# A two-exponential wait becomes a one-exponential wait in front of a row half's first MLP matmul

## The chip, the cores and the metric

The kernel runs on one core of one Trainium2 chip. The metric is the device time of one execution in microseconds (us), the median of several runs. The engines are TensorE (PE, its weight loads shown as PEld), VectorE (DVE), ScalarE (ACT), GpSimd (POOL) and SyncE (SP, which issues the DMAs).

## What is computed

One transformer-like block over 2048 rows of width 512, all in float32. The layer-normed input goes two ways, and the two results are multiplied:

```python
xn = _layernorm(x)
qkv = xn @ wqkv                                # 32 heads of width 16
p = softmax(q @ k.T * 16 ** -0.5)              # per head, 2048 x 2048
s = (p @ v) @ wo
h = relu(xn @ w1 + b1) ** 2                    # 512 -> 1792
g = silu(h @ w2 + b2)                          # 1792 -> 512
out = x + s * g
```

## The kernel before

**Stages.** Layer norm and the q, k, v projections come first (until about 374 us of the profile). Then a loop runs over 512 steps (`NU * 16`). A step handles four heads, 512 queries and 128 keys: four score matmuls (line 1161, tile `se`) into a ring of three PSUM banks, four exponentials on ScalarE (line 1167, tiles `pt` and `ex`), and, two steps later, four matmuls of the exponentials with v (line 374, tile `po`), which the profile shows as eight. Sixteen steps make a unit; 32 units make the attention.

**Work beside it.** The softmax shift of a unit is taken from row maxima that are computed ahead of it: score matmuls of another orientation (line 300, tile `pm_t`, a ring of three banks) and a VectorE reduction for each (line 308, tile `mx`). The MLP and afterwards the `wo` projection are handed out to the steps as small pieces by the generator `dense()`. Float32 accuracy is kept by splitting each operand into a high and a low part and doing three matmuls per product (`terms3`).

**Row halves.** A score matmul contracts over 64 partitions only, so it uses one half of the PE's rows: half 0 (partitions 0 to 63) or half 1 (64 to 127). An MLP matmul contracts over 128, so it is cut in two, one for each row half, and both accumulate into the same PSUM bank `pd_t`. The kernel first issues all of one half's MLP matmuls, each beside a matmul of the attention on the other half, and then all of the other half's, with the roles swapped. [...]

**Long blocks.** From the second of eight MLP chunks on, most MLP pieces come as blocks of 12 units for each row half (`block`, line 228): one unit is two matmuls of 256 columns in the first layer (`first_pair`, weights `w1s`) or one of 512 columns in the second (`second`, weights `w2t`). `long_slots` spreads one block over four steps, two for each half, and writes PE's order out by hand: the PE, ScalarE, VectorE, GpSimd and SP queues all keep the order in which the code issues. `visit(h, mine, theirs)` reads two strings of letters, one for the half that does the MLP and one for the other: `D` is an MLP unit, `s` a score matmul with its exponential, `m` a row-maximum matmul with its reduction.

There are two forms of a half. If the row maxima are far enough ahead (`ahead_m`), it is `s`, 12 times `D`, `s`, then both steps' matmuls with v together. Otherwise it is 10 times `D`, a step's matmuls with v, then `D D s s`, then the other step's matmuls with v. The counters of the code give which form is used: of the 88 long blocks the first 54 take the first form, and the 34 from step 292 on take the second. In the profile the second form runs from about 1020 us to 1478 us.

**The recording.** In `visit`, each `s` of the half that has no `D` left is recorded in `last_use[0]`, so the last one stays. In the first form that is one exponential. In the second it is the second of the two behind the last `D`.

**Who uses it.** In each of the 34 blocks the first MLP matmul of half 1. Where the block does not end its accumulation (13 of the 34), the recorded exponential is also used by the first MLP matmul of the next block, or of the next single slot (`halves`, line 190; three of the 13). Where it ends it, `post` sends the bank to ScalarE (line 545: bias and relu of the first layer; line 566: copy of the second), `last_use[0]` is cleared, and the next block's first MLP matmul waits for that evacuation of the single bank `pd_t` instead.

Of the kernel before, what the change touches and what calls it, by code (L numbers as in the profile page):

```python
# [39 lines left out]
def kernel(  # L40
# [55 lines left out]
    with ExitStack() as ph:  # L96
# [80 lines left out]
        last_use = [None]  # L177
# [110 lines left out]
        def max_mm(j, spread=False):  # L288
            if not m_ready(j, 1):
                return None  # L290
            u, p, qb, kc = todo_m[j].pop(0)
            qd = u // 4
            if u not in mxs:
                mxs[u] = sp.tile([P, 16, 4], F32, name="mx")
            m_bank[0] += 1
            if spread and m_bank[0] % 2:
                ps = pe.tile([P, 512], F32, name="se")
            else:
                ps = pm.tile([P, 512], F32, name="pm_t")
            nc.tensor.matmul(  # L300
                ps,
                qms[u][p][64 * j : 64 * j + 64, qb * P : (qb + 1) * P],
                kas[qd, p][64 * j : 64 * j + 64, kc * 512 : (kc + 1) * 512],
                start=True, stop=True,
            )
            c = (2 * p + j) * 4 + qb
            done_m[j] += 1
            return nc.vector.tensor_reduce(  # L308
                mxs[u][:, c, kc : kc + 1], ps, axis=AX.X, op=ALU.max
            )  # L310
# [3 lines left out]
        def max_end():  # L314
            while steps[0] < sum(done_m) // 4:
                u, s = divmod(steps[0], 16)
                if s == 15 and min(done_m) < 32 * (u + 1):
                    return
                steps[0] += 1
                if s in (9, 11) and u + 1 < NU:  # L320
                    assert min(done_m) >= 32 * u + 16
                    load_q_pair(u + 1, "qm", (s - 9) // 2, qms.setdefault(u + 1, []))
                if s == 15:
                    m4 = sp.tile([P, 16], F32, name="m4")
                    nc.vector.tensor_reduce(m4, mxs[u], axis=AX.X, op=ALU.max)
                    mxs[u] = m4
                    late.append((now[0] + 2, u))

        def shift_due():
            if late and late[0][0] <= now[0]:  # L330
                shift(late.pop(0)[1])
# [821 lines left out]
        def exp_mm(st, j, pts, spare):  # L1153
            u, kb = divmod(st, 16)
            qd = u // 4
            b = 64 * (j % 2)
            if spare:
                se = pm.tile([P, 512], F32, name="pm_t")
            else:
                se = pe.tile([P, 512], F32, name="se")  # L1160
            nc.tensor.matmul(  # L1161
                se, kas[qd, j // 2][b : b + 64, kb * P : (kb + 1) * P],
                qes[u][j // 2][b : b + 64, :],
                start=True, stop=True,
            )
            pts[j] = free_pt.pop(0)
            return nc.scalar.activation(pts[j], se, AF.Exp, scale=0.25)  # L1167
# [3 lines left out]
        def pv_step(st, pts):  # L1171
            u, kb = divmod(st, 16)
            if kb == 0:
                pos[0] = pv.tile([P, 512], F32, name="po")
            pv_mm(pos[0], u // 4, kb, pts)
            free_pt.extend(t for _, t in sorted(pts.items()) if all(t is not x for x in gone_pt))
            if kb == NT - 1:
                if u < NU - 2:
                    evac(pos[0], u)
                elif u == NU - 2:  # L1180
                    unit_inner(pos[0])
                else:
                    unit_final(pos[0])
# [57 lines left out]
        def ahead_m(n, st):  # L1241
            wo0 = 16 * NU - 62
            for u in range(n // 64, NU):
                end = 16 * u - SHIFT
                n_max = n + 4 * max(0, end - st)
                n_max += max(0, min(end, wo0 + 32) - max(st, wo0))
                if n_max < 64 * (u + 1):
                    return False
            return True

        def long_slots(st0, units, post):

            todo = [[(st0 + k, j) for k in range(4) for j in (lane, lane + 2)] for lane in range(2)]
            for kb in range(st0, st0 + 4):
                pts.setdefault(kb, {})

            def s(lane):
                kb, j = todo[lane].pop(0)
                return exp_mm(kb, j, pts[kb], False)

            def visit(h, mine, theirs):
                own, other, use = units[h], 1 - h, None
                for i, ops in enumerate(zip(mine, theirs)):
                    for lane in (other, h):
                        o = ops[0] if lane == h else ops[1]
                        if o == "D":
                            own.pop(0)()
                        elif o == "m":
                            max_mm(lane)
                        elif o == "s":  # L1270
                            use = s(lane)
                            if lane == h and not own:
                                last_use[0] = use

            for h in range(2):
                st = st0 + 2 * h
                if st > st0:
                    begin(st)
                if ahead_m(sum(done_m) + 7, st + 2):
                    visit(h, "s" + "D" * 12 + "s", ".mmsmssmsmssmm")  # L1280
                    if h and post is not None:
                        post()
                    begin(st + 1)
                    max_end()
                    shift_due()
                    for kb in (st - 2, st - 1):
                        pv_step(kb, pts.pop(kb))
                else:
                    visit(h, "D" * 10, "msmsmsmsms")
                    max_end()  # L1290
                    shift_due()
                    pv_step(st - 2, pts.pop(st - 2))
                    begin(st + 1)
                    visit(h, "DDss", "mmsm")
                    if h and post is not None:
                        post()
                    max_end()
                    shift_due()
                    pv_step(st - 1, pts.pop(st - 1))
            if post is not None:  # L1300
                last_use[0] = None
            assert not todo[0] and not todo[1] and not units[0] and not units[1]
# [17 lines left out]
        def begin(st):  # L1320
            now[0] = st
            if st % 64 == 48 and st // 64 + 1 < NQ:
                load_v(st // 64 + 1)
            if st >= 64 and st % 64 < 6 and st // 64 + 1 < NQ:
                for n in range(2):
                    load_k(st // 64 + 1, 2 * (st % 64) + n)
            u, s = divmod(st + 16, 16)
            if 2 <= u < NU and s < 2:
                load_q_pair(u, "qe", s, qes.setdefault(u, []))
            run_waiting()  # L1330
# [56 lines left out]
```

## Time and profile before

| | |
|---|---|
| median of 3 runs | 1728.29 us (1727.36 to 1729.73) |
| the profiled execution | 1729.29 us |
| its span, first to last instruction | 1727.5 us |
| PE busy | 97% of the span |
| VectorE, ScalarE, GpSimd busy | 78%, 69%, 31% |
| granted TensorE clock, mean | 0.998 |

A line of the grouped views names the source line, the engine, the operation and the tiles (out<-in), then count, busy time and mean duration. In a timeline a row has the start in us from the span's start, the length, engine, line, operation, tiles, shapes and how many alike instructions were merged; in brackets stands how long that engine sat idle before and what released it. Matmuls are pipelined: a 512-column matmul is shown for 0.39 to 0.50 us although the next one of the same row half can start 0.23 us after it. So "busy" says that some matmul is in flight, not that both row halves are.

### The profile page before, as it was taken

Reading aid. Unit: us, or ns where it says so; the run is one execution under the profiler, and the core shown is the slowest. Engines: PE = TensorE matmul, PEld = TensorE weight load, DVE = VectorE, ACT = ScalarE, POOL = GpSimd, SP = SyncE. Lnnn points to the kernel's source line nnn. Section 1 sums busy time; section 2 is a strip of 40 time slices with the busy share of each in tenths; the row PEclk is TensorE's granted clock in tenths of the full one; section 3 lists DMA queues with packets and bytes.
Section 4 is the critical chain, followed back from the end, with each engine's and each line's share of the span. In section 5 each row is a group of like instructions: output and inputs, shape, how many; then the busy total and the mean of one; then the engine's idle time right before and its main releaser. Section 6 shows DMA issues by size and latency. Waiting matters only on the chain.

```text
span 1727.5 us, 35413 instructions
## 1 busy us (share of the span) xinstructions
PE 1671.6 (97%) x13296; PEld 997.1 (58%) x13296; DVE 1340.1 (78%) x2294; ACT 1194.8 (69%) x2354; POOL 528.9 (31%) x548
## 2 busy tenths in 40 slices
PE   6999999999999999999999999999999999999997
PEld 4766666556656655665665565555555555555533
DVE  6599988887787788778777877887788778888612
ACT  6211377778778777877787776676767766776585
POOL 4434567523212312321232122112310223133433
PEclk9999999999999999999999999999999999999999
DMA  7567455436232522553244333233315332157344
GB/s 275 168 214 232 168 174 171 118 93 164 59 98 88 129 75 69 149 118 88 61 130 93 87 112 88 77 100 92 96 56 118 87 104 54 38 188 204 101 146 137
DMA packets 156723, 208.00 MB, mean 120 GB/s; under 512 B 51272, under 2 KB 71240, under 8 KB 155016
## 3 DMA queue, kind: packets, MB, share of 16 engines
q1 hardware_dynamic: 156552, 205.74, 41.0%
q8 instruction: 105, 1.72, 0.4%
q14 instruction: 66, 0.54, 0.1%
HBM read 149.30 MB, written 56.09 MB: 119 GB/s over the span
## 4 chain that ended last, share of the span: by engine, by line
PE 84%; issue 4%; ACT 3%; POOL 2%; DVE 2%; DMA 2%; SPq 1%; POOLq 0%; ACTq 0%; DVEq 0%
PE po L374 24%; PE pd_t L234 17%; PE pm_t L300 14%; PE se L1161 12%; PE pd_t L202 6%; PE pd_t L936 2%; PE po L936 2%; DVE mx L308 2%; ACT pt L1167 2%; PE se L300 2%; PE se L967 1%; ACT r L545 1%; PE se L936 1%; PE po L967 1%; PE pd_t L967 1%
## 5 line engine op out<-in xcount | busy, mean ns | idle before, releaser
L308 DVE TENSOR_REDUCE mx<-pm_t 128x1 f32<-128x512 f32 x1946 | 1212.0, 682 | 266.0 <-PE pm_t L300 150.8
L1167 ACT ACTIVATE pt<-se 128x512 f32<-128x512 f32 x1721 | 909.7, 611 | 297.3 <-PE se L1161 213.7
L1161 PE MATMUL se<-qe,ka 64*128 64x512 f32 x1988 | 764.7, 423 | 2.0 <-ACT ex L1167 1.0
L300 PE MATMUL pm_t<-ka,qm 64*128 64x512 f32 x1946 | 737.9, 416 | 3.7 <-DVE mx L308 3.3
L374 PE MATMUL po<-pt,v 128*32 128x512 f32 x3562 | 522.2, 602 | 0.0
L300 PEld LDWEIGHTS pm_t<-ka,qm 64*128 64x128 f32 x1946 | 341.4, 184 | 215.3 <-DVE mx L308 198.2
L1161 PEld LDWEIGHTS se<-qe,ka 64*128 64x128 f32 x1988 | 352.7, 184 | 128.0 <-ACT pt L1167 56.8
L234 PE MATMUL pd_t<-xc,w1s 64*128 64x256 f32 x2352 | 317.7, 285 | 12.4 <-ACT r L545 11.4
L234 PEld LDWEIGHTS pd_t<-xc,w1s 64*128 64x128 f32 x2352 | 296.4, 187 | 25.4 <-ACT r L545 16.5
L234 PE MATMUL pd_t<-w2t,hT 64*128 64x512 f32 x936 | 247.5, 402 | 3.1 <-ACT r L545 2.4
L374 PE MATMUL po<-ex,v 128*32 128x512 f32 x534 | 204.8, 601 | 0.0
L1167 ACT ACTIVATE ex<-se 128x512 f32<-128x512 f32 x267 | 157.9, 611 | 54.3 <-PE se L1161 32.0
L374 PEld LDWEIGHTS po<-pt,v 128*32 128x32 f32 x3562 | 90.7, 108 | 157.2 <-issue 139.7
L234 PEld LDWEIGHTS pd_t<-w2t,hT 64*128 64x128 f32 x936 | 164.1, 184 | 20.7 <-issue 4.8
L548 POOL TENSOR_TENSOR r<-r 128x512 f32<-128x512 f32 x49 | 51.0, 1040 | 362.8 <-ACT r L545 362.7
L567 POOL TENSOR_TENSOR u<-u,b_t 128x512 f32<-128x512 f32 x16 | 20.6, 1286 | 301.2 <-ACT u L566 301.2
L202 PE MATMUL pd_t<-w2t,hT 64*128 64x512 f32 x408 | 105.6, 391 | 0.3
L412 POOL TENSOR_TENSOR ot<-ot,hl 128x512 f32<-128x512 f32 x31 | 39.8, 1283 | 199.1 <-DMA hl<-r_d 141.0
L202 PE MATMUL pd_t<-wot,oc 64*128 64x512 f32 x336 | 90.9, 406 | 8.7 <-DVE mx L308 6.2
L202 PEld LDWEIGHTS pd_t<-wot,oc 64*128 64x128 f32 x336 | 58.4, 184 | 58.3 <-ACT pt L1167 16.0
L308 DVE TENSOR_REDUCE mx<-se 128x1 f32<-128x512 f32 x102 | 69.6, 683 | 15.5 <-PE se L300 8.0
L202 PEld LDWEIGHTS pd_t<-w2t,hT 64*128 64x128 f32 x408 | 72.5, 184 | 10.7 <-issue 1.1
(125 smaller groups left out, 1227.8 us busy)
## 6 DMA issues: line engine op xcount, KB each, us to landing
w1s<-w_d SPq DMA_DIRECT2D x196, 256.0 KB
qm<-q_d SPq DMA_DIRECT2D x384, 32.0 KB
qe<-q_d SPq DMA_DIRECT2D x384, 32.0 KB
ka<-k_d SPq DMA_DIRECT2D x96, 128.0 KB
xn_d<-xT SPq DMA_DIRECT2D x8, 1024.0 KB
k_d<-hl SPq DMA_DIRECT2D x32, 256.0 KB
q_d<-hl SPq DMA_DIRECT2D x32, 256.0 KB
xc<-xn_d SPq DMA_DIRECT2D x16, 512.0 KB
```

What stands on the lines that cost most here:

```text
L202: mm = nc.tensor.matmul(out_, lh(r), rh(r), start=first_ and lane == 0, stop=last_ and lane == 1, skip_group_check=True,)
L234: mm = nc.tensor.matmul(out_, lh(r), rh(r), start=first_ and lane == 0, stop=last_ and lane == 1, skip_group_check=True,)
L300: nc.tensor.matmul(ps, qms[u][p][64 * j : 64 * j + 64, qb * P : (qb + 1) * P], kas[qd, p][64 * j : 64 * j + 64, kc * 512 : (kc + 1) * 512] ...
L308: return nc.vector.tensor_reduce(mxs[u][:, c, kc : kc + 1], ps, axis=AX.X, op=ALU.max)
L374: nc.tensor.matmul(po[32 * j : 32 * j + 32, :], vs[qd][:, (4 * kb + j) * VW : (4 * kb + j) * VW + 32], pts[j], start=(kb == 0), stop=(kb = ...
L412: nc.gpsimd.tensor_tensor(ot, ot, hl[:, 1].bitcast(F32), op=ALU.mult)
L548: nc.gpsimd.tensor_tensor(r, r, r, op=ALU.mult)
L567: nc.gpsimd.tensor_tensor(u, u, b2_t, op=ALU.add)
L936: nc.tensor.matmul(out_, lh(slice(0, P)), rh(slice(0, P)), start=first_, stop=last_)
L967: nc.tensor.matmul(out_, lh(slice(0, P)), rh(slice(0, P)), start=first_, stop=last_)
L1161: nc.tensor.matmul(se, kas[qd, j // 2][b : b + 64, kb * P : (kb + 1) * P], qes[u][j // 2][b : b + 64, :], start=True, stop=True,)
L1167: return nc.scalar.activation(pts[j], se, AF.Exp, scale=0.25)
```

## The change

Only the recording in `visit` changes. Behind the last `D`, the first `s` of that half is recorded and later ones are not. The order of instructions on every engine stays as it is.

```diff
             def visit(h, mine, theirs):
-                own, other, use = units[h], 1 - h, None
+                own, other, follow = units[h], 1 - h, True
                 for i, ops in enumerate(zip(mine, theirs)):
...
                         elif o == "s":
                             use = s(lane)
-                            if lane == h and not own:
-                                last_use[0] = use
+                            if lane == h and not own and follow:
+                                last_use[0], follow = use, False
```

## The prediction

> **What bounds the kernel now.** First the page and the two stages of the MLP, cut where the second form of a half begins.
>
> ```profile
> span 1727.5 us, 35413 instructions
> PE 1671.6 (97%) x13296; PEld 997.1 (58%) x13296; DVE 1340.1 (78%) x2294; ACT 1194.8 (69%) x2354; POOL 528.9 (31%) x548
> PE 84%; issue 4%; ACT 3%; POOL 2%; DVE 2%; DMA 2%; SPq 1%; POOLq 0%; ACTq 0%; DVEq 0%
> ...
> 374.00:1020.00 646.00, 642.57 (x5725) 397.19 (x5727) 512.12 (x873) 509.22 (x1019) 158.72 (x156) 1.00 0.37 100
> 1020.00:1478.00 458.00, 441.52 (x3647) 248.00 (x3640) 370.65 (x614) 322.30 (x635) 107.63 (x107) 1.00 0.33 89
> ```
>
> PE is the bound (97% busy, 84% of the chain), and in the stage that the change touches it shows 441.5 of 458 us busy. VectorE has 87 us to spare there, ScalarE 136. Read like this, at most 16 us of PE idle time are to be had. But busy means that one matmul is in flight; whether both row halves work is not in that number. So next the waits of PE's weight loads in the stage, and then a transition in order of time.
>
> ```profile
> PEld pd_t L234 <- ACT r L545: 16.5, 16, 1.0
> PEld pd_t L234 <- ACT pt L1167: 7.5, 24, 0.3
> PEld pd_t L234 <- ACT ex L1167: 1.6, 5, 0.3
> ```
>
> 29 times a weight load of an MLP matmul waits for an exponential, 0.3 us each. The change's wait is there, and it is not covered. Here is one, in the second layer:
>
> ```profile
> 1151.57 1.57 ACT L1167 ACTIVATE pt<-se 128x512 f32<-128x512 f32 x3 [1.34 <-PE se L1161]
> 1151.70 1.07 PE L374 MATMUL po<-pt,v 128*32 128x512 f32 x8
> 1152.69 0.50 PE L300 MATMUL pm_t<-ka,qm 64*128 64x512 f32 x1
> 1153.19 0.18 PEld L234 LDWEIGHTS pd_t<-w2t,hT 64*128 64x128 f32 x1 [0.32 <-ACT pt L1167]
> 1153.20 0.50 PE L234 MATMUL pd_t<-w2t,hT 64*128 64x512 f32 x1
> 1153.20 0.49 PE L1161 MATMUL se<-qe,ka 64*128 64x512 f32 x1
> 1153.54 0.39 PE L234 MATMUL pd_t<-w2t,hT 64*128 64x512 f32 x1
> ...
> 1155.37 0.39 PE L234 MATMUL pd_t<-w2t,hT 64*128 64x512 f32 x1
> 1155.69 0.64 PE L374 MATMUL po<-pt,v 128*32 128x512 f32 x4
> ```
>
> Three exponentials stand in ScalarE's queue: one of the other half, then the first and the second own one. They end at 1153.14. The matmuls with v (1151.70) are over; a row-maximum matmul, m1, starts on the one half at 1152.69; the MLP's first matmul, D1, starts on the other at 1153.20, 0.05 us after the last exponential. For 0.51 us one half of the array has no work, and PE counts as busy all the while, since m1 is shown for 0.50 us. Behind D1 in PE's queue stands the next score matmul, which comes out with it. From D1 on the ten MLP matmuls run at their own pace (1153.54 to 1155.37 is 8 x 0.23 us), and the next matmuls with v start 2.49 us after D1.
>
> **The change part by part.** Nothing is added, removed or reordered on any engine or DMA queue. 47 semaphore waits are lowered by one exponential: in each of the 34 blocks from step 292 on the first matmul of half 1, and 13 first matmuls of what follows a block that leaves its accumulation open. When the first own exponential ends is in the same rows: three took 1.57 us, one alone takes 0.60 (row below), so they end 0.49 us apart and the first own one at 1152.65. D1 could start at 1152.70, with m1. What that is worth differs by place: 29 plain ones, as the two waits count them; nine of the 34 in which a unit ends (every fourth block) and its transpose is in front; nine with a second wait.
>
> ```profile
> 1202.83 0.60 ACT L1167 ACTIVATE ex<-se 128x512 f32<-128x512 f32 x1 [1.40 <-PE se L1161]
> 1203.32 1.08 ACT L1167 ACTIVATE pt<-se 128x512 f32<-128x512 f32 x2
> 1203.96 0.50 PE L300 MATMUL pm_t<-ka,qm 64*128 64x512 f32 x1
> 1204.45 0.38 PE L234 MATMUL pd_t<-xc,w1s 64*128 64x256 f32 x1
> 1207.02 0.62 PE L374 MATMUL po<-pt,v 128*32 128x512 f32 x1
> ...
> 1189.71 1.58 ACT L1167 ACTIVATE pt<-se 128x512 f32<-128x512 f32 x3 [1.41 <-PE se L1161]
> 1191.20 0.50 PE L300 MATMUL pm_t<-ka,qm 64*128 64x512 f32 x1
> 1191.34 0.38 PE L234 MATMUL pd_t<-xc,w1s 64*128 64x256 f32 x1
> 1193.42 0.39 PE L1161 MATMUL se<-qe,ka 64*128 64x512 f32 x1
> 1193.92 0.64 PE L374 MATMUL po<-pt,v 128*32 128x512 f32 x4
> ```
>
> *First layer, D1 0.49 us behind m1: 15 places.* The two transitions above are a test that the kernel makes by itself. In the second, a transpose in front holds m1 back, so that D1 comes only 0.14 us behind it. From D1 to the matmuls with v it is 2.57 us in the one and 2.58 in the other: the stretch does not care how long D1 waited, it only begins later. The first own exponential ends at 1203.92 (1203.32 + 0.60), so D1 can start at 1203.97, 0.48 us earlier. 15 x 0.48 = 7.2 us.
>
> *First layer, 0.14 us behind: 4 places.* There the first own exponential is long done, and D1 goes with m1: 4 x 0.13 = 0.5 us.
>
> *Second layer, 0.50 us behind: 14 places.* The matmuls are longer here, and the attention's half becomes the later one. m5, the fifth row maximum of the stretch, needs the bank that m2's reduction frees:
>
> ```profile
> 1153.23 3.25 DVE L308 TENSOR_REDUCE mx<-pm_t 128x1 f32<-128x512 f32 x5 [0.24 <-PE pm_t L300]
> ...
> 1140.82 0.50 PE L300 MATMUL pm_t<-ka,qm 64*128 64x512 f32 x1
> 1140.96 0.50 PE L234 MATMUL pd_t<-w2t,hT 64*128 64x512 f32 x1
> 1143.47 0.64 PE L374 MATMUL po<-pt,v 128*32 128x512 f32 x4
> ```
>
> Five reductions take 3.25 us, 0.65 each at most, and m1's starts at 1153.23, 0.54 us behind m1, so m2's is over 1.84 us behind m1. m5 loads its weights then at the earliest, and a last score matmul follows it: in the first-layer place with 0.14 us, where this half already runs without the delay, that score matmul starts 2.22 us behind m1 (1193.42 less 1191.20). From the last matmul of a half to those with v it is 0.32 us (1155.37 to 1155.69). So they cannot start before 2.54 us behind m1. Now it is 3.00 (1152.69 to 1155.69): 0.46 us each, 14 x 0.46 = 6.4 us. The bound from the other side is the 0.14 us place of the second layer, 2.65 us (1140.82 to 1143.47); if nothing can get under that, it is 0.35 each.
>
> *Second layer, 0.14 us behind: 5 places.* 2.65 to 2.54 is 0.11 at best, 0 by the same doubt; 5 x 0.1 = 0.5 us.
>
> *Nine places with a second wait.* The first matmul of a block that follows an open accumulation, and of three single slots:
>
> ```profile
> 1109.89 1.08 ACT L1167 ACTIVATE pt<-se 128x512 f32<-128x512 f32 x2
> 1110.52 0.50 PE L300 MATMUL pm_t<-ka,qm 64*128 64x512 f32 x1
> 1111.12 0.47 PE L234 MATMUL pd_t<-w2t,hT 64*128 64x512 f32 x1
> ...
> 1113.58 0.63 PE L374 MATMUL po<-pt,v 128*32 128x512 f32 x3
> ...
> 1122.81 0.49 PE L1161 MATMUL se<-qe,ka 64*128 64x512 f32 x1
> 1123.40 0.47 PE L202 MATMUL pd_t<-w2t,hT 64*128 64x512 f32 x1
> ```
>
> D1 comes 0.60 us behind its neighbour, 0.15 us after the exponential's end (1110.97) instead of 0.05: a separate wait in PE's queue costs the 0.1, and it stays. The first own exponential ends at 1110.49, so D1 moves to 1110.64, 0.48 us. The start of the matmuls with v falls from 3.06 us behind m1 to 2.58, above the 2.54. 9 x 0.48 = 4.3 us (0.40 each if 2.65 is the floor).
>
> *The added wait.* A later score matmul that reuses the bank of the second exponential had that wait implied by D1's and now needs its own. It is the third one of the next stretch, over 1.2 us behind m1, and the exponential is done 0.45 us behind m1 (1153.14 less 1152.69): nothing, as long as it fits into the matmul. If it costs a separate wait each time, 47 x 0.1 = 4.7 us. The row above shows such a separate wait. [...]
>
> Sum: 7.2 + 0.5 + 6.4 + 0.5 + 4.3 = 18.9 us. Against the profiled execution's 1729.3 us that gives 1710.4. It lies 1.0 us over the median of the runs, 1728.3, from which it gives 1709.4.
>
> **What is late next.** VectorE's 87 spare us of this stage shrink to about 68, which still leaves it behind PE. At D1 of half 0 of the first layer the relu holds as before:
>
> ```profile
> 1209.02 1.58 ACT L1167 ACTIVATE pt<-se 128x512 f32<-128x512 f32 x3 [1.39 <-PE se L1161]
> 1210.46 0.85 ACT L545 ACTIVATE r<-pd_t,b_t 128x256 f32<-128x256 f32 x2
> 1211.37 0.38 PE L234 MATMUL pd_t<-xc,w1s 64*128 64x256 f32 x1 [0.71 <-ACT r L545]
> ```
>
> **The rivals.** *Given back at the relu.* 19 first-layer places are followed by this wait for the relu. If ScalarE were behind, it would end at the same time as before and swallow 7.7 of the 18.9 us: 1717.1 us. Against it: ScalarE sat idle for 1.39 us before those exponentials, waiting for PE, so the relu moves with PE.
>
> *Another wait ends at the same time.* If D1 were also held by something else that ends with the second exponential, the change would do nothing: 1728.3 us. Against it: D1 comes 0.05 us after ScalarE in the plain places, whether m1 is 0.14 or 0.49 us ahead.
>
> *Slower, by the clock.* [...] If the granted clock fell in this stage, its 441.5 us would stretch: at 0.94 by 28 us, so 1737 us. It decides at 18.9 / 441.5, a clock under 0.96. Against it: the stage before has PE at 642.6 of 646 us and a clock of 1.00. [...]
>
> **How the numbers follow.** The forecast, a gain of 12 to 21 us, 0.86; given back at the relu 0.08; no effect 0.03; slower by the clock 0.03. Likeliest 1709.4 us. Lower end: every delay goes whole, 29 x 0.50 + 9 x 0.14 + 9 x 0.60 = 21.2 us, 1707.1, and 1.1 us for the spread of the runs shown: 1706.0. Upper end: second layer at its floor (14 x 0.35, nothing for the five, 9 x 0.40) 4.9 + 3.6 + 7.7 = 16.2 us, less 4.7 for separate waits, is 1716.8; it takes the relu rival in: 1717.5. Faster by over 0.2% (3.5 us, about what a measurement of this kernel can tell from no change): 0.86 + 0.08 = 0.94; same 0.03; slower 0.03.
>
> **What the profile after would show.** The 29 waits for exponentials at line 234 gone from the weight loads; D1 within 0.02 us of m1 in the plain places and about 0.1 in the nine; from m1 to the matmuls with v about 2.58 us in the first layer and 2.54 in the second; PE's busy time of the stage down by some 18 us with its idle time hardly changed; the relu waits as long as before. The prediction is wrong if D1 still comes 0.05 us after ScalarE's last exponential, if relu or reduction waits grow by what D1 gained, or if the clock drops.

## The result, and the profile after

The changed kernel takes 1711.82 us (median of 4 runs, 1710.34 to 1712.72), against 1728.72 us (four runs of the kernel before, 1727.36 to 1729.73): ratio 0.9902, 95% interval 0.9885 to 0.9919. The profiled execution after took 1710.34 us, span 1708.6 us. That is 18.9 us less span than before.

First the head of the page, its chain line and the two stages of the MLP. The second stage, cut at 1478 us before, is cut at 1461 us here; the columns are stretch, length, busy time of PE, its weight loads, VectorE, ScalarE and GpSimd, granted clock, DMA share, GB/s.

```profile
span 1708.6 us, 35413 instructions
PE 1655.0 (97%) x13296; PEld 987.1 (58%) x13296; DVE 1337.6 (78%) x2294; ACT 1193.0 (70%) x2354; POOL 528.9 (31%) x548
PE 82%; issue 5%; ACT 3%; POOL 3%; DMA 3%; DVE 2%; SPq 1%; POOLq 0%; ACTq 0%; DVEq 0%
...
374.00:1020.00 646.00, 643.34 (x5729) 397.29 (x5729) 512.96 (x874) 509.94 (x1021) 158.82 (x156) 1.00 0.37 100
1020.00:1461.00 441.00, 425.42 (x3659) 238.57 (x3655) 368.66 (x615) 321.60 (x636) 107.62 (x107) 1.00 0.34 93
```

The stage without the change stands as it did. In the stage with it PE's busy time fell by 16.1 us (441.5 to 425.4) and its idle time from 16.5 to 15.6 us: the time came out of what the page calls busy. Next the waits of the MLP's weight loads in that stage.

```profile
PEld pd_t L234 <- ACT r L545: 16.5, 16, 1.0
...
PEld pd_t L234 <- issue: 3.3, 3, 1.1
...
PEld pd_t L234 <- ACT u L566: 1.6, 2, 0.8
```

The two rows with 29 waits for exponentials are gone. The 16 waits for the relu are as long as before. Now the timeline: a first-layer place, then one in the second layer (with two of its weight loads), then one with a second wait.

```profile
1195.02 0.40 PE L234 MATMUL pd_t<-xc,w1s 64*128 64x256 f32 x2
...
1195.67 0.60 ACT L1167 ACTIVATE ex<-se 128x512 f32<-128x512 f32 x1 [1.41 <-PE se L1161]
1196.16 1.08 ACT L1167 ACTIVATE pt<-se 128x512 f32<-128x512 f32 x2
1196.81 0.49 PE L300 MATMUL pm_t<-ka,qm 64*128 64x512 f32 x1
1196.81 0.50 PE L234 MATMUL pd_t<-xc,w1s 64*128 64x256 f32 x2
1199.39 0.62 PE L374 MATMUL po<-pt,v 128*32 128x512 f32 x1
...
1147.52 0.49 PE L300 MATMUL pm_t<-ka,qm 64*128 64x512 f32 x1
1147.53 0.18 PEld L234 LDWEIGHTS pd_t<-w2t,hT 64*128 64x128 f32 x1
1147.53 0.49 PE L234 MATMUL pd_t<-w2t,hT 64*128 64x512 f32 x1
1149.39 0.18 PEld L300 LDWEIGHTS pm_t<-ka,qm 64*128 64x128 f32 x1 [0.18 <-DVE mx L308]
...
1149.73 0.39 PE L1161 MATMUL se<-qe,ka 64*128 64x512 f32 x1
1149.73 0.38 PE L234 MATMUL pd_t<-w2t,hT 64*128 64x512 f32 x1
1150.05 0.64 PE L374 MATMUL po<-pt,v 128*32 128x512 f32 x4
...
1107.16 0.50 PE L300 MATMUL pm_t<-ka,qm 64*128 64x512 f32 x1
1107.23 0.18 PEld L234 LDWEIGHTS pd_t<-w2t,hT 64*128 64x128 f32 x1
1107.27 0.46 PE L234 MATMUL pd_t<-w2t,hT 64*128 64x512 f32 x1
1109.71 0.63 PE L374 MATMUL po<-pt,v 128*32 128x512 f32 x3
```

ScalarE's queue holds the same three exponentials, the last of which ends at 1197.24 (1196.16 + 1.08). D1 no longer cares: it starts at 1196.81 together with m1, 0.06 us behind the first own exponential (the first of the two in the second row, which ends at 1196.75). From m1 to the matmuls with v it is 2.58 us there, 2.53 in the second layer and 2.55 behind a second wait. In the second layer m5's weight load at 1149.39 now waits for a reduction, m2's, 1.87 us behind m1. The last score matmul behind it and the last MLP matmul start at the same time, at 1149.73: neither half is the later one any more.

The wait itself is the kernel's own: `emit` makes D1 depend on the exponential in `last_use[0]` (lines 208 and 240), whose score matmul is issued on the first half behind its last MLP matmul. In the first-layer place that last MLP matmul ends at 1195.42 (first row), 1.39 us before D1 starts. What would happen if both halves wrote `pd_t` at once was not shown: no run leaves the dependency out.

### The profile page after: what moved, and what is told of

The parts are those of the page before. It is cut to its first block, busy times and chain, and to the rows that moved or that the text cites. A ratio compares the mean times of both kernels' runs of the same rounds, so it can differ in the third digit from the quotient of the medians.

```text
span 1708.6 us, 35413 instructions
## 1 busy us (share of the span) xinstructions
PE 1655.0 (97%) x13296; PEld 987.1 (58%) x13296; DVE 1337.6 (78%) x2294; ACT 1193.0 (70%) x2354; POOL 528.9 (31%) x548
## 4 chain that ended last, share of the span: by engine, by line
PE 82%; issue 5%; ACT 3%; POOL 3%; DMA 3%; DVE 2%; SPq 1%; POOLq 0%; ACTq 0%; DVEq 0%
PE po L374 24%; PE pd_t L234 15%; PE pm_t L300 14%; PE se L1161 13%; PE pd_t L202 6%; PE pd_t L936 2%; PE po L936 2%; DVE mx L308 2%; ACT pt L1167 2%; PE se L300 2%; ACT r L545 1%; PE po L967 1%; PE pd_t L967 1%; POOL ts L751 1%; POOL ts L750 1%
## 5 line engine op out<-in xcount | busy, mean ns | idle before, releaser
L234 PEld LDWEIGHTS pd_t<-xc,w1s 64*128 64x128 f32 x2352 | 296.5, 187 | 20.9 <-ACT r L545 16.5
```

What stands on the lines that cost most here:

```text
L234: mm = nc.tensor.matmul(out_, lh(r), rh(r), start=first_ and lane == 0, stop=last_ and lane == 1, skip_group_check=True,)
```

## The experiments

The runs were made in two groups with 11 and 17 runs of the kernel before (medians 1731.15 and 1731.54 us); each ratio is to the runs of its own group.

**The change again.**

> The changed kernel as it is, to settle whether it gains 16.9 us (the medians of the runs shown) or 18.9 us (the two profiled spans, 1727.5 and 1708.6). Theory of the recorded sum: 18.9 us below before. Rival: some 2 us of it are taken back outside the profiled execution: 17 us. No effect is out already.

Measured: 1713.45 us, ratio 0.9900 (0.9887 to 0.9914), span of the profiled execution 1710.4 us. The result repeats. The span is 1.8 us longer than that of the first profile, and one row of VectorE's waits (line, releaser, us in total, times, longest) has that much. Here it is for after, then for this run:

```profile
DVE sm L398 <- DMA sm<-ot: 0.4, 1, 0.4
```

```profile
DVE sm L398 <- DMA sm<-ot: 2.2, 1, 2.2
```

A reciprocal of a unit's row sums (near step 390) stands in VectorE's queue in front of row-maximum reductions and waits for the DMA that rearranges the sums. How long depends on when that DMA lands; it was 0.7 us before.

**One layer at a time.** `block` hands on its units' kind (2 for a first-layer block, 1 for the second), and only one kind records the first exponential. For the first layer:

```diff
-                                last_use[0], follow = use, False
+                                last_use[0], follow = use, per != 2
```

> The earlier exponential is recorded in blocks of the first MLP layer alone; in the second layer the second exponential stays. Theory: 15 places x 0.48 and 4 x 0.13, so 7.7 us faster than before, about 1721 us; the places of the second layer keep 0.50 us between the row-maximum matmul and the first MLP matmul. Rival (what the first layer gains is given back at the relu behind it): no change, 1728.7 us.

Measured: 1724.12 us, ratio 0.9959 (0.9946 to 0.9971), so 7.1 us. In the trace D1's weight load comes 0.003 us behind m1's in the first layer's places on average and 0.46 us in the second's, as before. The second layer is the same edit with `per != 1`:

> The other part alone: only blocks of the second MLP layer record the earlier exponential. Theory: 14 x 0.46, 5 x 0.1 and 9 x 0.48, so 11.2 us faster than before, about 1717.5 us, and the two parts add up to the whole. Rival (the second layer is paced by the row-maximum reductions, 0.35 us a place): 8.5 us, about 1720 us.

Measured: 1720.75 us, ratio 0.9945 (0.9931 to 0.9958), so 9.5 us, with D1's weight load at 0.03 us in the second layer and 0.42 in the first. This is 1.7 us short of the expectation. The three single slots gave 0.5 us less than forecast (see below), and the trace has the reciprocal's wait there too, 0.9 us longer than before. In the waits of the weight loads each run keeps one half of the exponentials, first the first-layer run, then the other:

```profile
PEld pd_t L234 <- ACT pt L1167: 3.8, 12, 0.3
...
PEld pd_t L234 <- ACT ex L1167: 0.6, 2, 0.3
```

```profile
PEld pd_t L234 <- ACT pt L1167: 3.7, 12, 0.3
...
PEld pd_t L234 <- ACT ex L1167: 0.9, 3, 0.3
```

14 waits stay with the first layer done and 15 with the second: the plain places as the prediction divided them. 7.1 and 9.5 add up to 16.6 us, the whole change gave 17.3 in the same group. Within the intervals the two layers' gains add up.

**Half the delay, without the change.** The kernel before, with its other half's score matmul one letter earlier, so that all exponentials start about a matmul earlier. D1 still waits for the second own exponential.

```diff
-                    visit(h, "DDss", "mmsm")
+                    visit(h, "DDss", "msmm")
```

> The kernel before, still waiting for the second exponential, with one letter moved: in the last two MLP units of a half the other half's score matmul is issued one place, 0.23 us, earlier (m s m m for m m s m). Its exponential is first of the three in ScalarE's queue, so the second own one should end 0.23 us earlier. Theory (the price is the queue in front of the exponential that is waited for): the delay of the first MLP matmul falls from 0.49 to 0.26 us in 29 places, from 0.60 to 0.37 in nine and from 0.14 to 0 in nine: 9.9 us faster than before, about 1719 us. Rival (the price is the wait itself, a fixed latency between the engines): no change.

Measured: 1715.67 us, ratio 0.9912 (0.9898 to 0.9927), so 15.2 us, far more than expected. The delay itself did what was expected. First a first-layer place, then the wait for the relu in this run:

```profile
1197.63 1.08 ACT L1167 ACTIVATE pt<-se 128x512 f32<-128x512 f32 x2
1198.50 0.50 PE L300 MATMUL pm_t<-ka,qm 64*128 64x512 f32 x1
1198.76 0.38 PE L234 MATMUL pd_t<-xc,w1s 64*128 64x256 f32 x1
```

```profile
PEld pd_t L234 <- ACT r L545: 12.9, 16, 0.8
```

D1 is 0.26 us behind m1 where it was 0.49, and again 0.05 us behind the last exponential's end (1198.71). What the expectation left out: the relu stands behind the same exponentials in ScalarE's queue and came earlier too. Its waits fell from 16.5 to 12.9 us in 16 places, 0.23 us each. The stage has 21 transitions behind such an evacuation (19 of the relu, two of the copy at line 566). From m1 to the matmuls with v they became 4.8 us shorter in all, most of the missing 5.3.

**The same letter in the changed kernel.** If that reading holds, the letter is worth only the relu's part here.

> The changed kernel with the same letter moved as in the dose run on the kernel before. There the first MLP matmul no longer waits, so nothing is left to gain in the 47 places; but the relu stands behind the same three exponentials in ScalarE's queue, and what the dose run gained beyond the 9.9 us foreseen (15.2 measured) should come from there: 21 places x 0.23 us. Theory: 4.8 us faster than the changed kernel, so 22 us below the kernel before, ratio 0.987. Rival (moving the letter gains by something else in those units, the same in both kernels): 15 us below the changed kernel, ratio 0.981. Rival (nothing left to gain): 0.990.

Measured: 1707.98 us, ratio 0.9865 (0.9846 to 0.9883); the profiled span is 1704.4 us, 4.2 less than after. The waits of the MLP's weight loads:

```profile
PEld pd_t L234 <- ACT r L545: 12.8, 16, 0.8
...
PEld pd_t L234 <- issue: 2.6, 3, 0.9
...
PEld pd_t L234 <- ACT u L566: 1.2, 2, 0.6
```

These three rows were 16.5, 3.3 and 1.6 us after the change: 4.8 us less in 21 waits, of which the reciprocal takes back 0.9 (its wait is 1.3 us here). The reading holds.

**The letter the other way, in the kernel before.** `"mmms"` puts the other half's score matmul last.

> The kernel before with the other half's score matmul one place later instead (m m m s for m m s m). ScalarE's queue then holds first own, other, second own: the second own one is third as before and ends at the same time. Theory: no change, within 2 us of the kernel before, and the first MLP matmul stays 0.49 us behind the row-maximum matmul. Rival (any shift of that letter changes how the two halves pair up and so the time): over 4 us either way.

Measured: 1733.11 us, ratio 1.0006 (0.9996 to 1.0016): no change beyond the interval. In its trace D1 is 0.52 us behind m1 in the plain places of the first layer, where it was 0.49. So moving an `m` past that `s` brings nothing as such; what paid in the two runs before is that ScalarE started earlier.

**The relu in front of the last three exponentials, in the changed kernel.** The relu's wait is what the change left largest. Where a half ends its accumulation, `post()` moves in front of `"ss"`:

```diff
-                    visit(h, "DDss", "mmsm")
                     if h and post is not None:
+                        visit(h, "DD", "mm")
                         post()
+                        visit(h, "ss", "sm")
+                    else:
+                        visit(h, "DDss", "mmsm")
```

> The changed kernel with the evacuation of the MLP bank (relu, or the copy of the second layer) put into ScalarE's queue ahead of the three exponentials instead of behind them, where a block ends its accumulation; PE's order stays. It is not in the change; it tests whether the relu wait is the same kind of queue wait. Theory: the 1.2 us by which the first MLP matmul of the next block stands behind its neighbour go to zero in 19 places and 1.0 us in two, since the relu then ends over 1 us before that place: 24 us below the changed kernel, ratio about 0.976. Rival (the exponentials, now 0.85 us later, hold the score matmuls of the next block back by their three banks): half of it or less, ratio 0.983 or more.

Measured: 1689.3 us, ratio 0.9758 (0.9737 to 0.9778), 42 us faster than the kernel before and some 25 us faster than the changed one (0.9902 less 0.9758, of 1731.5): it beats both. First the relu's place after the change, then in this run:

```profile
1201.88 1.08 ACT L1167 ACTIVATE pt<-se 128x512 f32<-128x512 f32 x2
1202.52 0.50 PE L300 MATMUL pm_t<-ka,qm 64*128 64x512 f32 x1
1202.83 0.85 ACT L545 ACTIVATE r<-pd_t,b_t 128x256 f32<-128x256 f32 x2
1203.74 0.38 PE L234 MATMUL pd_t<-xc,w1s 64*128 64x256 f32 x1 [0.72 <-ACT r L545]
```

```profile
1188.82 0.84 ACT L545 ACTIVATE r<-pd_t,b_t 128x256 f32<-128x256 f32 x2 [1.09 <-PE pd_t L234]
1189.55 1.09 ACT L1167 ACTIVATE pt<-se 128x512 f32<-128x512 f32 x2
1190.08 0.49 PE L300 MATMUL pm_t<-ka,qm 64*128 64x512 f32 x1
1190.09 0.38 PE L234 MATMUL pd_t<-xc,w1s 64*128 64x256 f32 x1
```

After the change D1 follows the relu, 1.22 us behind m1. Here the relu runs ahead of the exponentials, at a time when ScalarE had been idle: after the change it waited 1.23 us for a score matmul there, and now it is still idle for 1.09 us in front of the relu, until the MLP matmuls are done. The relu is over 0.4 us before m1, and D1 starts with m1. 21 such transitions by 1.2 us are 25 us. The stretch from the first to the last of the 47 places is 23.1 us shorter than after; the rest is about what the reciprocal takes, whose wait is 2.4 us in this run and not 0.4.

**The reciprocal one step later, in the changed kernel.** All but the first and last piece of a unit's end are due one step later, to give the sums' DMA more time.

```diff
-EVAC = (1, 4, 5, 7, 9, 12)
+EVAC = (1, 5, 6, 8, 10, 12)
```

> The changed kernel with the reciprocal of a unit's row sums, and what follows it, one step later. In the second profile of the changed kernel VectorE waits 2.2 us at one place (step 390) for the DMA that brings the row sums, and the row-maximum matmuls behind it are 1.6 us late; in the kernel before the steps are longer and it waits 0.7 us. Theory: that wait goes, and the gain over the kernel before is the whole 18.9 us in all runs: 1 to 2 us below the changed kernel, ratio about 0.989. Rival (that wait costs PE nothing on the average): the same as the changed kernel, 0.990.

Measured: 1719.5 us, ratio 0.9928 (0.9911 to 0.9944): slower than the changed kernel (its fastest run, 1716.2, lies above seven of the eight of that kernel), so this expectation was wrong. Near step 390 the wait is gone as meant; earlier, from 300 to 1020 us, it grew. First after, then this run:

```profile
DVE sm L398 <- DMA sm<-ot: 2.2, 1, 2.2
```

```profile
DVE sm L398 <- DMA sm<-ot: 7.7, 2, 3.9
```

Why, in the waits of SP's queue around the new wait (895 to 946 us; 895 to 936 for after), again first after and then this run:

```profile
SPq L421 <- POOL hl L414: 7.9, 1, 7.9
```

```profile
SPq L421 <- POOL hl L414: 15.0, 1, 15.0
```

The normalization on GpSimd of the unit before is one of the pieces that were put off, and SP waits with the store of its result (line 421). Everything behind that store was late, the sums' DMA too: it was issued 10.0 us after ScalarE's copy that makes its input began (930.1 to 940.1), not 4.6 us (925.4 to 930.0). So the reciprocal got its step and lost more than that. Against the profile after, PE's matmuls fall back by 1.8 and 2.7 us at the two waits (near 584 and 944 us). The first wait costs 1.1 us more: PE was busy for only 1.1 of the 3.3 us from 582.0 on, and in the 3.4 us behind it (585.4 to 588.8) its granted clock is 0.50. Another 1.6 us are lost near 330 us, where PE waits for weights (`w2t`) that GpSimd splits behind a normalization, which started at 325.2 us and not at 320.8. The median is some 5 us above the changed kernel; how much of it each of these losses makes was not separated, and moving the reciprocal alone was not tried.

## Why the prediction was right

The predicted time was 1709.4 us, the measured one is 1711.8, inside the range, and the profiled executions differ by the forecast 18.9 us. By the terms of the sum, each measured in the trace as the change from m1 to the matmuls with v, place by place:

| term | predicted | measured |
|---|---|---|
| first layer, D1 0.49 us behind m1, 15 places | 7.2 | 7.2 |
| first layer, 0.14 us, 4 places | 0.5 | 0.5 |
| second layer, 0.50 us, 14 places | 6.4 | 6.3 |
| second layer, 0.14 us, 5 places | 0.5 | 0.5 |
| second wait: six blocks | 2.9 (6 x 0.48) | 3.1 |
| second wait: three single slots | 1.4 (3 x 0.48) | 0.9 |
| added wait of the third score matmul | 0 | 0 |

That is 18.5 us in the 47 places. The other 0.4 lies ahead of the first place and behind the last.

*The bound.* That PE's 16 us of idle time are not the limit was right, and it is the main reading: in the stretch from the first to the last place (1020.9 to 1479.6 us before, 1020.6 to 1460.9 after) busy time fell by 17.5 us and idle time by 0.9.

*The floor of the second layer* was right in size: 2.53 to 2.55 us in its plain places, against 2.54 forecast. The weight load of m5 waits for m2's reduction in all 14, as the prediction had it. But the attention's half did not become the later one: the last matmul of each half starts 0.32 to 0.34 us ahead of the matmuls with v, so the MLP's half ends at the same time. That the reduction sets the floor is therefore not shown; the ten MLP matmuls end no earlier. The bound from the other side, 2.65, was no floor: its five places went below it as well.

*The nine places* were right in kind and mis-sized in three. The separate wait stayed (in the trace a semaphore instruction stands in front of D1's weight load in all nine, before and after); D1's weight load comes 0.08 us behind m1 in the blocks and 0.11 in the single slots. But in a single slot D1's half was not idle all that time. Before (the score matmul at 1122.81 and D1 at 1123.40 stand in the prediction) and after:

```profile
1122.80 0.50 PE L300 MATMUL pm_t<-ka,qm 64*128 64x512 f32 x1
...
1124.99 0.62 PE L374 MATMUL po<-pt,v 128*32 128x512 f32 x2
```

```profile
1118.50 0.49 PE L300 MATMUL pm_t<-ka,qm 64*128 64x512 f32 x1
1118.50 0.49 PE L1161 MATMUL se<-qe,ka 64*128 64x512 f32 x1
1118.61 0.19 PEld L202 LDWEIGHTS pd_t<-w2t,hT 64*128 64x128 f32 x1
1118.83 0.39 PE L202 MATMUL pd_t<-w2t,hT 64*128 64x512 f32 x1
...
1120.38 1.07 PE L374 MATMUL po<-pt,v 128*32 128x512 f32 x8
```

A score matmul stands in front of D1. D1's weights load 0.11 us behind it, but the matmul starts 0.33 us behind it; from m1 to the matmuls with v the slot falls from 2.19 to 1.88 us, 0.31 and not 0.48.

*The added wait* is there and costs nothing that can be seen. That it would fit into the matmul was the author's assumption. In the trace's records the weight load of the third score matmul carries a wait for ScalarE in all 47 places, where it carried none before, and no semaphore instruction was added (35413 instructions in both profiles).

*The rivals.* "Given back at the relu" is out: the row with 16 waits is 16.5 us before and after, and ScalarE still sits idle for 1.41 us ahead of the exponentials. "Another wait ends at the same time" is out by the half-delay run, in which D1 followed the second exponential's end by 0.05 us at a new place. "Slower, by the clock" is out: the granted clock of the stage is 1.00.

*What it missed.* Under "what is late next" stood VectorE's spare time (72 us now, 68 forecast) and the relu. The reciprocal, behind a DMA, wasn't named. Its wait was 0.4 us in the profiled execution and 1.8 us more in another one.

*The 2.4 us between 1711.8 and 1709.4.* The 18.9 us were taken from a median of three runs, 1728.3, which later runs of the same kernel put at 1728.7, 1731.2 and 1731.5 in their groups. Of the single runs, those of equal granted clock can be compared: at 0.998 the four of before in the first group are 1729.3 to 1731.4 us (mean 1730.4), the two of the changed kernel 1711.9 and 1712.2, and that is 18.4 us. That what is left over belongs to the clock and the reciprocal is argued from their size, not shown.

## What to carry to other kernels

Where matmuls of two row halves run side by side, a busy PE doesn't mean two busy halves (before the change m1 ran alone for 0.49 to 0.50 us in 29 places here): look in the timeline for a matmul that starts alone, take how late its partner comes, and count the places. A dependency that stands for "the other half is done" should name the earliest instruction that proves it, and its price is the place of that instruction in its engine's queue (here one exponential earlier was 0.49 us); what else stands in that queue, here the relu, may cost more than the wait that one came for. And a step that is put off moves what it feeds in every queue behind it: 1 step for the reciprocal made the sums' DMA, behind a store in SP's queue, 5 us later.

## What the runs showed of the hardware

Of the runs of one kernel, those with a lower granted clock took longer on the average (for the kernel before in the second group 1731.1 us at 0.998, 1733.2 at 0.997, 1734.0 at 0.996), but not each of them (one at 0.996 took 1731.0). Here are a stretch of the first stage and the last one of the kernel after, and then the first again in the run with the early relu, whose profiled execution (1696.6 us) was the slowest of its four; the granted clock is the third number from the end:

```profile
60.00:80.00 20.00, 19.07 (x86) 13.33 (x85) 13.18 (x22) 4.47 (x7) 9.96 (x8) 1.00 0.77 202
...
1690.00:1708.00 18.00, 10.32 (x54) 6.31 (x53) 6.82 (x12) 3.52 (x8) 3.27 (x3) 0.82 0.38 132
```

```profile
60.00:80.00 20.00, 17.82 (x67) 12.30 (x66) 8.21 (x14) 3.98 (x7) 9.56 (x9) 0.83 0.76 182
```

At the end the clock drops in both kernels (0.82 here, 0.83 before), in the first stage only in some executions: a mean of 0.83 in 20 us is at most 3.4 us lost. The trace's records of the clock show it as stretches of 3.4 or 6.8 us at half speed (0.50), in the first stage, where PE is idle for 2.2 of the 20 us above, and near the end of the kernel; the run with the late reciprocal has one more, at 585.4 us, right behind its wait there. One such stretch of 3.4 us costs at most 1.7 us, or 0.001 of the kernel's mean clock. Runs at 0.996 are some 3 to 5 us slower than runs at 0.998 (1716.6, a single run, against 1712.0 us for the changed kernel; 1734.0 against 1731.1 for the kernel before in the second group). In the 3.4 us ahead of such stretches PE was not idle all of the time: it was busy for 1.1 us (late reciprocal), for 1.4 and 1.6 us (the first two of the run with the early relu) and for 1.6 us (the kernel after, from 1694.7 to 1698.1 us). What lowers the clock was not shown.
